# Attention inputs laid out by superchunk, with coarser routing steps and fp32 place tables

## The chip, the cores and the metric

The kernel runs on one core of a Trainium2 chip. A core has TensorE (matmuls), VectorE, ScalarE and GpSimd (elementwise work, each with its own queue of instructions), and SyncE (SP), which here only issues loads. The metric is the device time in microseconds; three runs of the kernel before gave 750.98, 752.05 and 753.02 us, median 752.05.

## The reference

Eight batches of 576 tokens with eight heads of 64 go through sliding-window attention, and each of the 4608 rows that come out (512 numbers) goes through one of eight experts. Which one depends on the token before it: a token keeps its predecessor's expert unless it is the first of its sequence or a local gate is below one half.

```python
mask = (rel >= 0) & (rel < 64)
scores = np.where(mask, scale * np.matmul(q, k.transpose(0, 1, 3, 2)), -1e9)
attn = softmax(scores)                      # per row
x = np.matmul(attn, v)                      # (B, S, H*D) after the bridge
logits = x @ w_gate                         # (B, S, 8)
local_gate = sigmoid(x @ w_local)           # (B, S)
# for each batch, token after token:
e = argmax(logits[b, s]) if s == 0 or local_gate[b, s] < 0.5 else prev_e
p = softmax(logits[b, s])
out[b, s] = p[e] * (relu(x[b, s] @ w1[e]) @ w2[e])      # 512 -> 1024 -> 512
```

All arithmetic is fp32.

## The kernel before, in words

**Attention** works on nine superchunks of 512 tokens (index `sc`), each with four head pairs (`hp`): 36 units. A unit is `scores` (L232 on: matmuls of keys against queries into PSUM, an exponential on ScalarE at L254, a multiplication p\*mask on VectorE at L257) and, two units later (LEAD = 2), `values` (L260 on: p against the values, L267; then on VectorE a reciprocal L272, the gate columns g L274 and the rows x L276). Once a superchunk, `gates` (L204) multiplies the transposed values `vtt` by the gate weights (L209), and `spread` (L215) transposes the result (L219) and puts it into the columns behind each head's values in `va` (L220), so that the value matmuls give the gate logits as well. Windows that start in the middle of a block of 128 need a second copy of the values shifted by 64 rows, `vb`; ScalarE makes it with five copies (L224, L227 to L230), two of them per unit.

**Loads** are issued on SP. `load(sc)` (L159) brings keys and queries into one tile of the pool `ring` (four buffers of 2 MB, which later hold expert weights) and the values into `va` (three buffers); `turned(sc)` (L171) brings `vtt` (one buffer). In memory, keys, queries and transposed values are [128, 4, 4608], so that a superchunk is four rows of 2 KB per partition; `v3` is [4608, 8, 74], four rows of 2368 B per partition. At the end of a superchunk, GpSimd issues the write of x to `xs` in memory (L322) and VectorE sums the gate columns into `lt` (L320).

**Routing** (`Router`) is written as generators that are advanced step by step between other work. `gate` (L554) does half of the tokens: argmax, the scan over tokens (transposes, scans on VectorE, transposes back), counts by matmuls with `ones` and `tri` (L628, L629), ranks. `first` (L734) then places the first half's tokens into six blocks of 128 and `second` (L766) all the rest into eight blocks of 256 and up to 21 of 128. `table` (L695) turns places into lists of tokens and weights: VectorE builds one-hot matrices for nine chunks of 128 tokens at a time (rowh L706; one L711; colh L716), TensorE multiplies them (L723), VectorE reads out `idx` and `pw` (L726 to L732). Before, the one-hot matrices are bf16; a token's number is split into two bf16 values and its weight into three (L656 to L659), five columns of values in all, and summed again at the end.

Each `yield` of these generators carries an estimate of VectorE's microseconds and whether a matmul follows that needs them. In attention, `step()` (twice a unit) advances `first` only when the estimate has been worked off at 0.8 us per call (HALF). In the experts, `step()` works off 3.5 us per call (STEP) and, when the account is empty, advances `second` up to the next matmul.

**Experts** (`Experts.run`, L897 on) go through 32 blocks: six of `first` (these are called quiet; ScalarE does all their PSUM reading), then 26 of `second`. `fetch` (L826) loads a block's two weight matrices (2 MB each, SP, L846) and gathers its rows (GpSimd, L840); `turn` transposes the rows (L859, L860), `hidden` does the first layer (L872) with the relu (L876, L878), `result` the second (L886), the scaling (L891) and the scattered write (L892). A step is taken after each group of `hidden` and twice per slot of `result`. A block is fetched two blocks ahead. Up to three more blocks may be needed; they are fetched and computed inside a conditional at the end, which these inputs do not enter.

**Order.** TensorE's instructions run as written (`manual_schedule`); the other engines' queues are ordered by the framework's scheduler, by priority in program order among what it takes to be ready. Each engine then runs its queue in order.

Of the kernel before, what the change touches and what calls it, by code (L numbers as in the profile page):

```python
# [11 lines left out]
BF16 = mybir.dt.bfloat16  # L12
# [7 lines left out]
P = 128  # L20
# [34 lines left out]
HALF = 0.8  # L55
STEP = 3.5
# [5 lines left out]
def kernel(  # L62
# [4 lines left out]
    v: bass.AP,  # L67
    v3: bass.AP,
# [30 lines left out]
    with ExitStack() as fast:  # L99
        ring = fast.enter_context(tc.tile_pool(name="ring", bufs=4))  # L100
        rt = Router(fast, tc, lt, tabs, ident)
        ex = Experts(fast, tc, ring, *moe)
        attention(tc, ring, q, k, v3, vt, xs, lt, ok, wg2s, ident, rt, ex)
        ex.run(fast, rt)
# [31 lines left out]
def attention(ctx, tc, ring, q, k, v3, vt, xs, lt, ok, wg2, ident, rt, ex):  # L136
# [22 lines left out]
    def load(sc):  # L159
        t = slice(sc * SC, (sc + 1) * SC)  # L160
# [4 lines left out]
        for i in range(0, HP, step):  # L165
            h = slice(i, i + step)
            nc.sync.dma_start(out=kt[:, h], in_=k[:, h, t])
            nc.sync.dma_start(out=qt[:, h], in_=q[:, h, t])
        nc.sync.dma_start(out=va, in_=v3[t].rearrange("(c p) h x -> p c h x", p=P))

    def turned(sc):  # L171
        vtt = vts[sc] = kp.tile([P, HP, SC], F32, name="vtt", bufs=1)
        nc.sync.dma_start(out=vtt, in_=vt[:, :, sc * SC:(sc + 1) * SC])
# [41 lines left out]
    def spread(sc, r, gs):  # L215
# [6 lines left out]
        vb = vbs[sc] = kp.tile([P, 4, H, VW], F32, name="vb", bufs=2)  # L222
        if sc:
            nc.scalar.copy(vb[WIN:, 0], vas[sc - 1][WIN:, 3])  # L224
        else:
            nc.gpsimd.memset(vb[WIN:, 0], 0.0)
        return [lambda: nc.scalar.copy(vb[:WIN, :2], va[:WIN, :2]),  # L227
                lambda: nc.scalar.copy(vb[WIN:, 1:3], va[WIN:, :2]),
                lambda: nc.scalar.copy(vb[:WIN, 2:], va[:WIN, 2:]),
                lambda: nc.scalar.copy(vb[WIN:, 3], va[WIN:, 2])]  # L230
# [50 lines left out]
    for move in spread(0, *gated):  # L281
        move()
    units = [(sc, hp) for sc in range(NSC) for hp in range(HP)]
    ps = {u: scores(*u) for u in units[:LEAD]}
    gated, moves = None, []
    side = None
    pause = 0

    def step():
        nonlocal pause  # L290
        if side and pause <= 0:
            pause = next(side, (0.0, False))[0]
        pause -= HALF

# [3 lines left out]
    for i, (sc, hp) in enumerate(units):  # L298
# [7 lines left out]
        if gated:  # L306
            moves = spread(sc + 1, *gated)
            gated = None
        for move in moves[:2]:
            move()  # L310
        moves = moves[2:]
        step()
# [5 lines left out]
        step()  # L318
# [173 lines left out]
class Router:  # L492
# [9 lines left out]
    def __init__(self, ctx, tc, lt, tabs, ident):  # L502
# [10 lines left out]
        self.iob = iota("iob", [1, NBLK, 1], [[1, NBLK], [0, 1]])  # L513
        pos = iota("pos", [P, G, GC], [[0, G], [P, GC]], 1)
# [14 lines left out]

        self.w = tl("w", P, C, 5, dt=BF16)  # L530
        nc.vector.tensor_copy(self.w[:, :, 0], iota("chunk", [P, C], [[1, C]], 0, -C))
        nc.vector.tensor_copy(self.w[:, :, 1], iota("at", [P, C], [[0, C]], 1))
# [21 lines left out]
    def gate(self, half, psum):  # L554

# [13 lines left out]
        yield 1.2, False  # L572
# [7 lines left out]
        yield 1.0, True  # L580
# [11 lines left out]
        yield 1.5, True  # L592
# [9 lines left out]
        yield 0.8, True  # L602
# [11 lines left out]
        yield 1.0, True  # L614
# [7 lines left out]
        yield 0.6, True  # L622
# [14 lines left out]
        yield 1.2, False  # L637
# [12 lines left out]
        yield 1.2, False  # L650
        pt = tl("pt", P, C1)
        vec.tensor_reduce(pt, pa, axis=AX.X, op=Alu.add)
        vec.tensor_tensor(pt, pt, sm, op=Alu.mult)

        w = self.w[:, cs]
        vec.tensor_copy(w[:, :, 2], pt)  # L656
        vec.tensor_tensor(pt, pt, w[:, :, 2], op=Alu.subtract)
        vec.tensor_copy(w[:, :, 3], pt)
        vec.tensor_tensor(w[:, :, 4], pt, w[:, :, 3], op=Alu.subtract)  # L659
# [35 lines left out]
    def table(self, psum, cs, ns, lo, hi, idx, pw):  # L695

        nc, last, vec = self.nc, self.last, self.nc.vector
# [3 lines left out]
        for a in range(0, n, 2 * m):  # L701
            built = []
            for b in range(a, min(a + 2 * m, n), m):
                rowh = self.oh_p.tile([P, m, P], BF16, name="rowh")
                sh = [P, m, P]
                vec.tensor_tensor(rowh, self.io128.to_broadcast(sh), last(lo[:, b:b + m]).to_broadcast(sh),  # L706
                                  op=Alu.is_equal)
                yield 1.3, False
                one = self.oh_p.tile([P, m, 1, NS], BF16, name="one")[:, :, :, :ns]
                sh = [P, m, ns]  # L710
                vec.tensor_tensor(one[:, :, 0], self.ios[:, :, :ns].to_broadcast(sh),  # L711
                                  last(hi[:, b:b + m]).to_broadcast(sh), op=Alu.is_equal)
                colh = self.oh_p.tile([P, m, 5, NS], BF16, name="colh")[:, :, :, :ns]
                sh = [P, m, 5, ns]
                w = self.w[:, cs.start + b:cs.start + b + m, :].rearrange("p c (k o) -> p c k o", o=1)
                vec.tensor_tensor(colh, one.to_broadcast(sh), w.to_broadcast(sh), op=Alu.mult)  # L716
                built.append((rowh, colh))
                yield 0.3 + 0.05 * ns, b + m >= min(a + 2 * m, n)
            if tab is None:
                tab = psum()[:, :5 * ns].rearrange("p (k s) -> p k s", k=5)  # L720
            for k, (rowh, colh) in enumerate(built):
                for i in range(m):
                    nc.tensor.matmul(tab, lhsT=rowh[:, i, :], rhs=colh[:, i], start=(a + k + i == 0),  # L723
                                     stop=(a + k * m + i == n - 1))
        t = self.tl("t", P, 5, NS)[:, :, :ns]
        vec.tensor_copy(t, tab)  # L726
        at = self.tl("at", P, NS)[:, :ns]
        vec.scalar_tensor_tensor(at, t[:, 0], float(P), t[:, 1], Alu.mult, Alu.add)
        vec.tensor_scalar(at, at, float(N), 0.0, Alu.add, Alu.max)
        vec.tensor_scalar(idx, at, float(N), None, Alu.min)  # L730
# [262 lines left out]
```

## Time and profile before

The profiled execution took 752.05 us; its span, from first to last instruction, is 750.2 us, at a mean granted TensorE clock of 0.981.

| | busy us | share of the span |
|---|---|---|
| TensorE matmuls | 691.8 | 92% |
| TensorE weight loads (beside them) | 502.4 | 67% |
| VectorE | 182.7 | 24% |
| ScalarE | 145.8 | 19% |
| GpSimd | 92.8 | 12% |

203.84 MB were moved. The busy share is an average over two stages of different kinds: attention (to 149 us), in which all engines work and the DMA engines are full, and the experts (161 to 742 us), in which TensorE never stops. A wait costs time only where it holds up the engine that sets the pace of its stage.

### The profile page before, as it was taken

Reading aid. Unit: us, or ns where it says so; the run is one execution under the profiler, and the core shown is the slowest. Engines: PE = TensorE matmul, PEld = TensorE weight load, DVE = VectorE, ACT = ScalarE, POOL = GpSimd, SP = SyncE. Lnnn points to the kernel's source line nnn. Section 1 sums busy time; section 2 is a strip of 40 time slices with the busy share of each in tenths; the row PEclk is TensorE's granted clock in tenths of the full one; section 3 lists DMA queues with packets and bytes.
Section 4 is the critical chain, followed back from the end, with each engine's and each line's share of the span. In section 5 each row is a group of like instructions: output and inputs, shape, how many; then the busy total and the mean of one; then the engine's idle time right before and its main releaser. Section 6 shows DMA issues by size and latency. Waiting matters only on the chain. (4 is left out here: it accounts for less than half of the span.)

```text
span 750.2 us, 12553 instructions
## 1 busy us (share of the span) xinstructions
PE 691.8 (92%) x5479; PEld 502.4 (67%) x5479; DVE 182.7 (24%) x426; ACT 145.8 (19%) x186; POOL 92.8 (12%) x109
## 2 busy tenths in 40 slices
PE   3788787749999999999999999999999999999995
PEld 2666666647677767567567567576776777677673
DVE  4576788923730011011010010010010001001000
ACT  2667665401111101101101101100110110010010
POOL 2000000111132111111110110111111111010010
PEclk9799999969999999999999999999999999999998
DMA  9999996867889964644654643689889898888601
GB/s 327 388 393 399 395 388 251 321 245 251 325 313 382 423 268 142 241 178 140 231 186 139 225 187 141 216 308 348 307 332 328 307 343 307 319 295 310 225 15 31
DMA packets 37331, 203.84 MB, mean 272 GB/s; under 512 B 3437, under 2 KB 3453, under 8 KB 29072
## 3 DMA queue, kind: packets, MB, share of 16 engines
q1 hardware_dynamic: 28320, 173.45, 63.1%
q0 software_dynamic: 8944, 29.45, 9.9%
q8 instruction: 47, 0.77, 0.4%
q14 instruction: 20, 0.16, 0.1%
HBM read 184.01 MB, written 19.92 MB: 272 GB/s over the span
## 5 line engine op out<-in xcount | busy, mean ns | idle before, releaser
L872 PEld LDWEIGHTS hp<-xt,w 128*128 128x128 f32 x2048 | 274.8, 193 | 28.3 <-issue 14.3
L872 PE MATMUL hp<-xt,w 128*128 128x128 f32 (+1 forms) x2048 | 289.9, 303 | 0.7 <-ACT xt L860 0.7
L886 PE MATMUL yp<-w,h 128*128 128x512 f32 x640 | 280.4, 592 | 0.0
L886 PEld LDWEIGHTS yp<-w,h 128*128 128x128 f32 x640 | 118.9, 190 | 136.8 <-issue 134.9
L876 DVE TENSOR_SCALAR h<-hp 128x512 f32<-128x512 f32 x34 | 23.5, 691 | 473.5 <-issue 362.0
L891 ACT ACTIVATE y<-yp,pw 128x512 f32<-128x512 f32 x40 | 27.5, 687 | 358.3 <-PE yp L886 342.2
L892 POOL DMA_INDIRECT out_dram<-y,idx x40 | 41.8, 1045 | 302.6 <-ACT y L891 275.8
L840 POOL DMA_INDIRECT xg<-xs,idx x40 | 39.1, 977 | 217.3 <-PE tp L859 188.4
L878 ACT ACTIVATE h<-hp 128x512 f32<-128x512 f32 x46 | 27.5, 597 | 163.0 <-PE hp L872 163.0
L238 PE MATMUL sp<-w 64*64 64x128 f32 (+1 forms) x1296 | 46.4, 278 | 13.7 <-issue 8.4
L238 PEld LDWEIGHTS sp<-w 64*64 64x64 f32 x1296 | 39.7, 142 | 22.8 <-issue 14.4
L267 PE MATMUL xo<-vb,p 128*64 128x74 f32 x576 | 46.8, 233 | 8.3 <-issue 4.3
L267 PEld LDWEIGHTS xo<-vb,p 128*64 128x64 f32 x576 | 40.8, 138 | 11.5 <-issue 4.8
L267 PE MATMUL xo<-va,p 128*64 128x74 f32 x576 | 47.0, 234 | 1.5 <-issue 1.5
L257 DVE TENSOR_TENSOR p<-p,mask 128x1024 f32<-128x1024 f32 x36 | 43.9, 1221 | 12.1 <-ACT p L254 11.9
L267 PEld LDWEIGHTS xo<-va,p 128*64 128x64 f32 x576 | 40.8, 138 | 2.7 <-issue 2.7
L254 ACT ACTIVATE p<-sp 128x1024 f32<-128x1024 f32 x36 | 36.7, 1022 | 15.7 <-PE sp L238 14.1
L859 PE MATMUL tp<-ident,xg 128*128 128x128 f32 x160 | 23.2, 277 | 10.8 <-DMA xg<-xs,idx 10.8
L859 PEld LDWEIGHTS tp<-ident,xg 128*128 128x128 f32 x160 | 18.9, 143 | 11.8 <-issue 11.0
L209 PE MATMUL xo<-vtt,wg2s 128*32 128x512 f32 x72 | 12.5, 705 | 13.9 <-DMA wg2s<-in_wg_dram 8.3
L276 DVE TENSOR_TENSOR x<-xo,allr 128x512 f32<-128x512 f32 x36 | 24.5, 680 | 0.0
L322 POOL DMA_DIRECT2D xs<-x x9 | 6.9, 764 | 130.3 <-DVE x L276 116.2
(198 smaller groups left out, 201.5 us busy)
## 6 DMA issues: line engine op xcount, KB each, us to landing
w<-in_w_dram SPq DMA_DIRECT2D x64, 2048.0 KB, 8.7
va<-in_v_dram SPq DMA_DIRECT2D x9, 1184.0 KB, 12.6
vtt<-in_vt_dram SPq DMA_DIRECT2D x9, 1024.0 KB, 11.1
xs<-x POOLq DMA_DIRECT2D x9, 1024.0 KB, 10.2
w<-in_k_dram SPq DMA_DIRECT2D x8, 1024.0 KB, 13.1
w<-in_q_dram SPq DMA_DIRECT2D x8, 1024.0 KB, 15.0
w<-in_k_dram SPq DMA_DIRECT2D x4, 256.0 KB, 6.1
w<-in_q_dram SPq DMA_DIRECT2D x4, 256.0 KB, 5.8
```

The source lines that it names most:

```text
L238: nc.tensor.matmul(sp[c * WIN:(c + 1) * WIN, j, a:b], lhsT=kt[h, hp, block * WIN:(block + 1) * WIN], rhs=qt[h, hp, a:b], start=True, stop= ...
L254: nc.scalar.activation(p, sp, Act.Exp, scale=DH ** -0.5)
L257: nc.vector.tensor_tensor(p, p, m.to_broadcast([P, 2, SC]), op=Alu.mult)
L267: nc.tensor.matmul(xo[par * WIN:(par + 1) * WIN, j, s * VW:(s + 1) * VW], lhsT=p[:, j, b * WIN:(b + 1) * WIN], rhs=w[:, s, 2 * hp + j, :], ...
L276: nc.vector.tensor_tensor(x[:, :, hp].rearrange("p c j d -> p j c d"), o[:, :, :, :DH], rr.to_broadcast([P, 2, 4, DH]), op=Alu.mult)
L840: nc.gpsimd.indirect_dma_start(out=x, out_offset=None, in_=self.xs[:rows, :], in_offset=bass.IndirectOffsetOnAxis(ap=idx[:, s:s + 1], axis=0))
L859: nc.tensor.transpose(tp[:, kk, :], x[:, kk * P:(kk + 1) * P], self.ident)
L872: nc.tensor.matmul(hp[:, i, :], lhsT=st["w1"][:, kk, m * P:(m + 1) * P], rhs=st["xt"][:, kk, :n], start=(kk == 0), stop=(kk == DK - 1))
L878: nc.scalar.activation(o, hp, Act.Relu)
L886: nc.tensor.matmul(yp, lhsT=st["h"][:, m, i * P:(i + 1) * P], rhs=st["w2"][:, m, :], start=(m == 0), stop=(m == FK - 1))
L891: nc.scalar.activation(y, yp, Act.Copy, scale=st["pw"][:, s:s + 1])
L892: nc.gpsimd.indirect_dma_start(out=self.out[:, :], out_offset=bass.IndirectOffsetOnAxis(ap=st["idx"][:, s:s + 1], axis=0), in_=y, in_offse ...
```

## The change

Four parts, in one diff.

1. Layout and loads. Keys and queries come as `kq`, [9, 128, 2, 4, 512]; values and transposed values are also laid out by superchunk. `load` issues one load for keys and queries (2 MB; for superchunk 0 four of 512 KB, one per head pair), with 16 KB in a row per partition, 9.5 KB for `va` and 8 KB for `vtt`. The plain `q`, `k`, `v` stay for the conditional part at the end of the kernel.
2. `vb` is copied by GpSimd in three copies right after `spread`, in place of ScalarE's five over two units.
3. Routing advances one `yield` at a time without accounts: in attention once per unit, in the experts at each call, the first of which now comes ahead of the first block's `turn`. There are fewer yields, only where a matmul follows or a large part ends. The one-hot matrices are fp32, with two columns of values (token, weight) in place of five; each piece takes one comparison for rowh, one for colh and two multiplications.
4. In the experts, blocks are fetched two ahead to the end of the list, and the three spare ones unconditionally; the conditional only computes them.

```diff
     def load(sc):
-        t = slice(sc * SC, (sc + 1) * SC)
         both = ring.tile([P, 2, HP, SC], F32, name="w")
...
-            nc.sync.dma_start(out=kt[:, h], in_=k[:, h, t])
-            nc.sync.dma_start(out=qt[:, h], in_=q[:, h, t])
-        nc.sync.dma_start(out=va, in_=v3[t].rearrange("(c p) h x -> p c h x", p=P))
+            nc.sync.dma_start(out=both[:, :, h], in_=kq[sc, :, :, h])
+        nc.sync.dma_start(out=va, in_=v3[sc])
...
-        nc.sync.dma_start(out=vtt, in_=vt[:, :, sc * SC:(sc + 1) * SC])
+        nc.sync.dma_start(out=vtt, in_=vt[sc])
...
+        nc.gpsimd.tensor_copy(vb[:WIN], va[:WIN])
+        nc.gpsimd.tensor_copy(vb[WIN:, 1:], va[WIN:, :3])
         if sc:
-            nc.scalar.copy(vb[WIN:, 0], vas[sc - 1][WIN:, 3])
+            nc.gpsimd.tensor_copy(vb[WIN:, 0], vas[sc - 1][WIN:, 3])
...
-        return [lambda: nc.scalar.copy(vb[:WIN, :2], va[:WIN, :2]),
-                lambda: nc.scalar.copy(vb[WIN:, 1:3], va[WIN:, :2]),
-                lambda: nc.scalar.copy(vb[:WIN, 2:], va[:WIN, 2:]),
-                lambda: nc.scalar.copy(vb[WIN:, 3], va[WIN:, 2])]
...
-        step()
         values(sc, hp, ps.pop((sc, hp)), x, g)
...
-        step()
+        if side:
+            next(side, None)
...
# Router.table, for each piece of nine chunks (each yield of gate, first and second loses its weights)
-                rowh = self.oh_p.tile([P, m, P], BF16, name="rowh")
+                rowh = self.oh_p.tile([P, m, P], F32, name="rowh")
...
-                colh = self.oh_p.tile([P, m, 5, NS], BF16, name="colh")[:, :, :, :ns]
-                vec.tensor_tensor(colh, one.to_broadcast(sh), w.to_broadcast(sh), op=Alu.mult)
-                yield 0.3 + 0.05 * ns, b + m >= min(a + 2 * m, n)
+                colh = self.oh_p.tile([P, m, 2, NS], F32, name="colh")
+                one = colh[:, :, 1, :ns]
+                eng.tensor_tensor(one, self.ios[:, :, :ns].to_broadcast(sh), last(hi[:, b:b + m]).to_broadcast(sh),
+                                  op=Alu.is_equal)
+                eng.tensor_tensor(colh[:, :, 0, :ns], one, last(self.tok[:, c]).to_broadcast(sh), op=Alu.mult)
+                eng.tensor_tensor(one, one, last(self.pt[:, c]).to_broadcast(sh), op=Alu.mult)
                 built.append((rowh, colh))
+            yield
...
# Experts.run
         def step():
-            nonlocal side, pause
-            pause -= STEP
-            if pause > 0.0:
-                return
-            pause, trip = 0.6, False
-            while side and not trip:
-                w, trip = next(side, (0.0, None))
-                pause += w
-                if trip is None:
-                    side = None
-                    late.append(self.fetch(0, spare=True))
+            nonlocal side
+            if side and next(side, self) is self:
+                side = None
+                late.append(self.fetch(0, spare=True))
...
-            n = order[i + 2] if i + 2 < total else 0
-            if n:
+            n = order[i + 2]
+            if n > 0 or n < 0:
                 jobs.append(self.fetch(n, spare=n > 0 and n % 3 == 0))
...
+        for n in order[total + 2:]:
+            jobs.append(self.fetch(n, spare=n % 3 == 0))
...
-            for n in order[total:]:
-                st = self.fetch(n, spare=n % 3 == 0)
+            for st in jobs[total:]:
                 self.turn(st, False)
```

## Prediction

> **What bounds the kernel now.** I read the 40 slices first, then ten-microsecond windows, TensorE's waits, and the timeline at the two seams. TensorE is busy 92% of the span and without a gap from 161 us to 742 us, so the expert stage is paid by TensorE alone: only what makes it wait there, or gives it more to do, counts. Attention (8 to 148.7 us) and the step into the experts (148.7 to 161.3 us) are where it idles.
>
> Windows; after the busy times of five engines come TensorE's granted clock, DMA share and GB/s:
>
> ```profile
> 50.00:60.00 10.00, 8.91 (x219) 6.91 (x214) 7.75 (x15) 5.98 (x7) 0.76 (x1) 1.00 1.05 395
> 120.00:130.00 10.00, 8.47 (x216) 6.83 (x215) 9.52 (x36) 6.12 (x8) 0.75 (x1) 1.00 0.46 149
> 240.00:250.00 10.00, 10.00 (x78) 8.97 (x77) 0.00 (x0) 2.85 (x5) 2.21 (x3) 1.00 1.01 431
> ```
>
> At 50 us the DMA engines are full at 395 GB/s with rows of 2 KB; at 240 us they are full with weight rows of 16 KB at 431 GB/s. From 120 us VectorE is the crowded engine (95%).
>
> But is attention late for data? What TensorE waited for from 40 to 95 us:
>
> ```profile
> PE xo L267 <- issue: 5.2, 4, 1.8
> PE sp L238 <- issue: 4.5, 4, 1.8
> PE xo L209 <- issue: 1.1, 1, 1.1
> PE xo L209 <- PE xo L267: 0.4, 1, 0.4
> ```
>
> No wait names a load. Nine gaps of "issue", 10.8 us, fall in the middle of runs of matmuls; otherwise the blocks touch (scores of a unit 1.05 us, values 1.19 us). So a superchunk is 10.6 us of TensorE (four units of 2.24, gates 1.0, transposes 0.6), 2.7 us of these gaps and some 0.4 of refilling after them: the 13.7 us between ends of superchunks.
>
> The seam to the experts, in the timeline:
>
> ```profile
> 146.34 0.62 PE L723 MATMUL xo<-colh,rowh 128*128 128x30 bf16 x18 [0.77 <-DVE x L276]
> 148.25 1.04 POOL L840 DMA_INDIRECT xg<-xs,idx  x1 [5.72 <-DVE idx L730]
> 159.50 1.08 PE L859 MATMUL tp<-ident,xg 128*128 128x128 f32 x4 [10.83 <-DMA xg<-xs,idx]
> 161.26 6.06 PE L872 MATMUL hp<-xt,w 128*128 128x128 f32 x32 [0.68 <-ACT xt L860]
> 167.37 3.74 PE L872 MATMUL hp<-xt,w 128*128 128x128 f32 x32
> ```
>
> The first place table is ready only in the last unit; its gather lands 11 us later beside weight loads, TensorE idles 10.83 us, and its clock then costs 6.06 - 3.74 = 2.3 us.
>
> The second routing, inside the experts:
>
> ```profile
> 182.76 0.41 PE L628 MATMUL r<-oh,ones 128*128 128x144 f32 x2
> 187.26 7.03 PE L886 MATMUL yp<-w,h 128*128 128x512 f32 x16
> 193.08 1.35 DVE L706 TENSOR_TENSOR rowh<-io,lo 128x1152 bf16<-128x1152 f32 x1
> 194.35 0.50 DVE L711 TENSOR_TENSOR one<-ios,hi 128x333 bf16<-128x333 f32 x1
> 205.15 1.64 PE L723 MATMUL r<-colh,rowh 128*128 128x185 bf16 x18
> ```
>
> VectorE needs until 193.1 us from the counts of 182.8 us to begin the table; the pauses put the table's matmuls at 205.2 us, well behind it.
>
> [...] 47 packets of 0.77 MB on the instruction queue, gaps roughly every 128 load-and-multiply pairs; so I read "issue" as instruction fetch beside full DMA engines. [...]
>
> **The change part by part**, against the profiled 752.05 us (span 750.2, 1.85 around it; its run is also the median of the three).
>
> *Loads.* Bytes per superchunk stay: 2048 + 1024 + 1184 KB in, 1024 KB of x out, 5.41 MB. At 395 GB/s that is 13.7 us, at about 425 (the rows out stay 2 KB) 12.7. So at most 1.0 us per superchunk, 5 us over the five before VectorE crowds. I take -1.0: no wait names data, and the fetch gaps were as long (0.72 and 1.29 us at 133 and 139 us) beside weight loads of 16 KB rows; the DMA engines stay nearly full at any pace TensorE can reach. Range -5 to +2[...]. One SP issue in place of two: 2.5 to 4 us less of SP per superchunk, but SP waits for buffers anyway; without that cover it would be 1 us of landing.
>
> *vb copies from ScalarE to GpSimd.* Three copies of 2368, 1776 and 592 elements. GpSimd's memset of 592 took 0.627 us, so I estimate 5.0 us in all per superchunk, against 4.9 on ScalarE. At the start ScalarE's copies (15.7 to 20.0 us) held the first exponential and TensorE for 5.38 us; values of unit 0 then began at 23.0. On GpSimd they end near 20.7, beside the exponentials: -1.8 (first gates load allowing; 0 to -2.3). Later they are due 8 us after va's columns: covered, but p*mask (1.22 us, two SBUF inputs) waits for a copy of up to 2.5 us. In superchunks 0 to 4 VectorE's 9.5 us of 13.7 and the lead of two units (3.5 us) cover it: +1.0 (0 to +3).
>
> *First routing, one step a unit.* Eight steps from unit 20 give the table at unit 27 of 36, not 35. VectorE's 17 us of routing (summed from L565 to L730 without the pieces removed) fall in two superchunks: 18.4 own + 17.0 + 5.0 for half of the GpSimd time blocked = 40.4, at the best share seen (95%) 42.5, less 3.5 of lead, against 31.4 between those ends before: +7.6. The last two superchunks lose their VectorE waits (2.4) and the table's matmuls (0.6): +4.6 net. Without blocking it is -0.6 (35.4 for 40.4); with all of it and more bubbles +10. f32 matmuls of the first table (36 records of at most 0.115 us) hide in those waits.
>
> *Seam.* Table, gather and both weights of the first block (buffers of superchunks 5 and 6, free at units 25 and 29) are in before attention ends, so tp, copy and hp follow at once, 1.3 us: -11.0, and a warm clock, -2.3. Together -13.3 (0 if the gather stays late). xs (row write of the last superchunk) and the second block's weights are due 14 us later.
>
> *Second routing, one step per call.* Calls come every 3.7 us as now until 182.8 us; then rest of gate, places and table take three calls. TensorE would want the first 18 table matmuls in the middle of result of block 2, 190.9 us. VectorE begins the table at 193.1 as before, and a piece is rowh 1.27 + three of 0.41 = 2.5 to 2.7 us: first piece 195.8, second 198.4. TensorE waits 5 us, does nine, waits 0.7, does nine: over at about 200.2, 9.3 us. The other half is ready in time: 3.2 us. An f32 table matmul is two records; 74 columns at the 0.88 ns per column of L886 are 0.065, at most the 0.115 us of L872's records, so 36 take 4.7 to 8.3, I take 6.4. Against 2 x 1.48 before: 12.5 - 2.95 = +9.6. [...] +2.3, as at the seam. +11.9 (8 to 15). Queued behind the waiting matmuls is all of TensorE's expert work, so nothing hides it. The bf16 splits (L656 to L659) go, but they fill VectorE's wait for L628: 0.
>
> *End.* Three spare blocks (12 MB, 3 gathers) are now fetched unconditionally. Every load needed is ahead of them on SP, and 4 MB per 14.45 us is the rate anyway: 0. But the last w2 waits for the last result's buffer (742.1 us) and lands 7.9 us later at best, with 0.3 for SP and 0.6 beside the last rows out, against a last landing near 750: +1.3 (0 to +4).
>
> Sum: -1.0 - 1.8 + 1.0 + 4.6 - 13.3 + 11.9 + 1.3 = +2.7, so 754.8 us.
>
> **Rivals.** (a) *GpSimd's copies hold VectorE throughout.* For: p*mask and most routing steps have two SBUF inputs. Against: half of VectorE's work reads PSUM. With all 5 us blocked a superchunk needs 14.5 us of VectorE, over 13.7: four superchunks at +0.8 and +4 more in the crowded two: 762. It decides from 4.2 us blocked per superchunk. (b) *Ends faster:* the copies block nothing (-0.6 in place of +4.6, 0 in place of +1.0: 748.6), at best with the loads' whole 5 us instead of 1: 744.6. I price it 746.5; it decides when less than about 1 us per superchunk is blocked. (c) *No change:* the loads give nothing, but TensorE keeps its clock in the table wait and the f32 matmuls run at the low price (+8 in place of +11.9): 751. (d) *The gather stays late,* queued on GpSimd behind x's writes: +13.3, 768. Against: two gathers were issued ahead of the last write before.
>
> **How the numbers follow.** This kernel's runs can't tell 0.3% (2.3 us) from no change: faster is below 749.8, slower above 754.3. Forecast 0.45 (own range 750 to 760: faster 0.03, same 0.15, slower 0.27); (a) 0.20 slower; (b) 0.20 faster; (c) 0.10 same; (d) 0.05 slower. So 0.23, 0.25, 0.52. From 746 to 764 leaves out half of (b) and all of (d) and the top of (a), about 0.2.
>
> **What would show it.** Right: tp (L859 before) within 2 us of the last values; one TensorE wait of 4 to 7 us on a VectorE piece of the table near 190 us and a slow stretch after it; GpSimd copies of about 2.5, 1.9 and 0.6 us; DMA near 420 GB/s in attention with "issue" gaps still there; a last w load landing after 749 us. Wrong: attention ending before 145 us (b) or after 156 us (a), p*mask stretched or late by copies; a gather landing after attention (d); no wait at the second table (c).

## The result, and the profile after

The changed kernel took 777.64 us (median of four runs, 776.95 to 779.68) against 751.51 us for the kernel before on the same chip. The ratio is 1.0355 with a 95% interval of 1.0321 to 1.0389: 24 to 29 us slower. The forecast was 754.8 us, range 746 to 764; the direction was right, the size far too small.

The profiled execution has a span of 775.2 us against 750.2 us. Both are divided at the same events (the first three rows are times from the span's start); the last matmul is the small transpose of a flag (L129 before, L127 after) that follows the last expert block.

| | before | after | difference |
|---|---|---|---|
| first gates matmul of superchunk 6 | 95.86 | 94.91 | -1.0 |
| attention's last values | 148.67 | 160.64 | +12.0 |
| first expert matmul | 161.26 | 161.85 | +0.6 |
| from there to the last matmul | 581.4 | 597.5 | +16.0 |
| from there to the span's end | 7.5 | 15.9 | +8.4 |
| span | 750.2 | 775.2 | +25.0 |

The same windows as before, with one more behind 120 us (busy time of five engines, TensorE's granted clock, DMA share, GB/s):

```profile
50.00:60.00 10.00, 9.16 (x236) 7.48 (x234) 7.38 (x14) 4.12 (x5) 4.45 (x3) 1.00 1.00 394
120.00:130.00 10.00, 1.21 (x32) 1.06 (x32) 9.96 (x34) 0.41 (x1) 1.43 (x2) 0.65 0.55 193
130.00:140.00 10.00, 9.52 (x72) 9.52 (x72) 1.52 (x9) 0.00 (x0) 0.43 (x1) 0.50 0.31 123
240.00:250.00 10.00, 10.00 (x75) 8.65 (x74) 0.00 (x0) 1.65 (x3) 1.00 (x1) 1.00 1.01 426
```

At 50 and 240 us little has changed. The loss of attention lies in one place: from 120 to 130 us TensorE works 1.2 of 10 us while VectorE is full, and from 130 to 140 us TensorE is "busy" at half clock with only 72 matmuls. (The trace's clock records have it at half from 122.9 to 143.4 us, and again from 194.6 to 208.2 us.) TensorE's timeline shows what that is, and the two other stages that the prediction priced:

```profile
130.48 7.83 PE L691 MATMUL xo<-colh,rowh 128*128 128x12 f32 x36 [9.27 <-DVE colh L683]
138.24 1.99 PE L232 MATMUL sp<-w 64*64 64x128 f32 x36
...
161.85 3.81 PE L834 MATMUL hp<-xt,w 128*128 128x128 f32 x32 [1.21 <-ACT xt L822]
...
195.85 7.93 PE L691 MATMUL r<-colh,rowh 128*128 128x74 f32 x36 [6.65 <-DVE colh L684]
203.58 5.96 PE L848 MATMUL yp<-w,h 128*128 128x512 f32 x8
209.38 4.14 PE L691 MATMUL r<-colh,rowh 128*128 128x74 f32 x36
```

The first table waits 9.27 us for VectorE's pieces, then takes 7.83 us where the bf16 table took 0.62, and a unit's scores after it take 1.99 us in place of 1.1. The seam is as forecast: the wait of 10.83 us for the gathered rows is gone, and the first 32 records take 3.81 in place of 6.06 us. The second table waits 6.65 us and takes 7.93 and 4.14 us.

The end, in the timeline of all engines, before:

```profile
742.42 0.27 PE L129 MATMUL op<-ident,ok 128*1 128x128 f32 x1 [0.30 <-PEq L946]
742.73 0.28 DVE L131 TENSOR_REDUCE lo<-op 1x1 f32<-1x128 f32 x1 [6.69 <-PE op L129]
```

and after:

```profile
759.04 0.27 PE L127 MATMUL op<-ident,ok 128*1 128x128 f32 x1 [0.64 <-PEq L901]
768.01 0.28 DVE L129 TENSOR_REDUCE lo<-op 1x1 f32<-1x128 f32 x1 [15.69 <-DMA w<-in_w_dram]
```

Before, VectorE reduces the flag 0.04 us after the matmul. After, it waits 8.7 us more, for the landing of the last spare block's weights; what follows the flag takes 7.5 us before and 7.2 us after. So the landing is in series with the flag. Why the flag's small tile waits for a tile of weights, the trace doesn't say. In the kernel its pool is opened after the experts' pools are closed, so it may stand in their place; no run tests that.

### The profile page after: what moved, and what is told of

It reads as the page before. It is cut to its first block, busy times and chain, and to the rows that moved or that the text cites. A ratio compares the mean times of both kernels' runs of the same rounds, so it can differ in the third digit from the quotient of the medians.

```text
span 775.2 us, 12649 instructions
## 1 busy us (share of the span) xinstructions
PE 708.4 (91%) x5533; PEld 517.8 (67%) x5533; DVE 186.8 (24%) x415; ACT 103.1 (13%) x142; POOL 152.1 (20%) x137
## 4 chain that ended last, share of the span: by engine, by line
PE 85%; DVE 7%; DMA 4%; issue 2%; ACT 0%; POOL 0%; DVEq 0%; POOLq 0%; ACTq 0%
PE hp L834 36%; PE yp L848 35%; PE sp L232 4%; PE xo L261 4%; PE tp L821 2%; DMA vtt<-in_vt_dram 2%; DVE p L251 2%; PE r L691 2%; PE xo L205 1%; DMA w<-in_w_dram 1%; PE xo L691 1%; DVE x L270 1%; DMA wg2s<-in_wg_dram 1%; DVE rowh L675 1%; PE xo L215 1%
## 5 line engine op out<-in xcount | busy, mean ns | idle before, releaser
L848 PE MATMUL yp<-w,h 128*128 128x512 f32 x640 | 282.8, 596 | 0.0
L848 PEld LDWEIGHTS yp<-w,h 128*128 128x128 f32 x640 | 119.9, 192 | 138.2 <-issue 136.3
L802 POOL DMA_INDIRECT xg<-xs,idx x43 | 42.1, 979 | 224.2 <-PE tp L821 199.9
L251 DVE TENSOR_TENSOR p<-p,mask 128x1024 f32<-128x1024 f32 x36 | 52.0, 1449 | 10.9 <-ACT p L248 10.7
L219 POOL COPY vb<-va 64x2368 f32<-64x2368 f32 x9 | 26.9, 2986 | 46.6 <-DVE va L216 46.6
L205 PE MATMUL xo<-vtt,wg2s 128*32 128x512 f32 x72 | 11.8, 736 | 13.3 <-DMA wg2s<-in_wg_dram 9.1
L822 DVE COPY xt<-tp 128x512 f32<-128x512 f32 x32 | 21.2, 680 | 0.0
```

The costliest lines, as they stand in the source:

```text
L251: nc.vector.tensor_tensor(p, p, m.to_broadcast([P, 2, SC]), op=Alu.mult)
L802: nc.gpsimd.indirect_dma_start(out=x, out_offset=None, in_=self.xs[:rows, :], in_offset=bass.IndirectOffsetOnAxis(ap=idx[:, s:s + 1], axis=0))
L848: nc.tensor.matmul(yp, lhsT=st["h"][:, m, i * P:(i + 1) * P], rhs=st["w2"][:, m, :], start=(m == 0), stop=(m == FK - 1))
```

## Experiments

Microseconds "by ratio" are (ratio - 1) x 752. The theory after these traces: four losses that are nearly separate, namely f32 tables on TensorE's path, VectorE's work handed over in large pieces, GpSimd's copies, and the fetches at the end; the layout gives nothing. The rival was the forecast's (a), GpSimd's lock on VectorE throughout.

**The layout alone**, put into the kernel before:

```diff
-            nc.sync.dma_start(out=kt[:, h], in_=k[:, h, t])
-            nc.sync.dma_start(out=qt[:, h], in_=q[:, h, t])
+            nc.sync.dma_start(out=both[:, :, h], in_=kq[sc, :, :, h])
# va and vtt as in the change, the arrays too
```

> The kernel before with only the new layout and the joined load of keys and queries. Account from the two traces: attention never waits for data, so 749 to 752 us, the fetch gaps of TensorE staying at about 2.7 us per superchunk. Rival (the loads set attention's pace): 746 us or less, with attention ending 5 us earlier. Rival (long rows delay instruction fetch): over 754 us, with longer gaps of 'issue'.

751.5 us, ratio 0.9985 (0.9969 to 1.0001): no change that can be told, at most 2.3 us of gain. From 50 to 90 us the DMA engines moved 411 GB/s in place of 396, and the gaps of "issue" from 40 to 95 us stayed (11.0 us against 10.8): attention did not wait for data, so data that comes sooner is worth nothing. That these gaps are instruction fetch, as the prediction reads them, is an estimate: the page of before has 12553 instructions and 47 packets on the instruction queue, 267 to a packet, near the 256 of 128 load-and-multiply pairs; no trace has the times of these packets.

**The spare fetches back inside the conditional**, in the kernel after:

```diff
-            n = order[i + 2]
-            if n > 0 or n < 0:
+            n = order[i + 2] if i + 2 < total else 0
+            if n:
...
-        for n in order[total + 2:]:
-            jobs.append(self.fetch(n, spare=n % 3 == 0))
...
-            for st in jobs[total:]:
+            for n in order[total:]:
+                st = self.fetch(n, spare=n % 3 == 0)
```

> The changed kernel with the three spare blocks fetched inside the conditional, as before. If the flag at the end waits for the last spare weight load, the time falls by the 8.7 us that the end grew, to 769 us, and the flag's reduction follows its transpose within 1 us. If the end is long for another reason (gathers, the drain), it falls by less than 3 us.

769.44 us, ratio 1.0252 (1.0214 to 1.0289). The flag's line is that of before again, in the timeline of this kernel:

```profile
758.25 0.28 DVE L129 TENSOR_REDUCE lo<-op 1x1 f32<-1x128 f32 x1 [6.69 <-PE op L127]
```

**The same part alone**, the fetches taken out of the conditional in the kernel before (the diff is the reverse):

> The kernel before with the spare weights fetched ahead of the conditional block and nothing else. If the flag's tile waits for the last weight's landing as it does in the kernel after: 15 to 18 us from the last matmul to the span's end in place of 8.1, and 758 to 761. If that loss needs the rest of the change: 751 to 753.

760.95 us, ratio 1.0113 (1.0081 to 1.0145), +8.5 by ratio. In its timeline:

```profile
743.08 0.27 PE L129 MATMUL op<-ident,ok 128*1 128x128 f32 x1 [0.61 <-PEq L948]
751.49 0.28 DVE L131 TENSOR_REDUCE lo<-op 1x1 f32<-1x128 f32 x1 [15.10 <-DMA w<-in_w_dram]
```

Put in or taken out, it is about 8 us, and nothing else of the change is needed for it. That it is shown both ways settles which part lengthens the end.

**Both tables' matmuls three steps later**, in the kernel after:

```diff
-            yield
+            for _ in range(wait if a == 0 else 1):
+                yield
# wait is a new argument of table(), 4 for both tables
```

> The changed kernel with three more yields between the building of each table's first pieces and the matmuls that read them; nothing else. If the two TensorE waits (9.3 and 6.7 us) and the half clock after them (about 7 and 6 us) are the loss, the time falls by 22 to 29 us, to 749 to 756 us, and the gather of the first block is still early. If the waits only move, because VectorE is short of time whatever the order (GpSimd's copies), it falls by less than 12 us, with a wait of similar length at the new place.

763.57 us, ratio 1.0160 (1.0127 to 1.0193). The second wait is gone and its two halves take 4.14 us each at full clock; first expert matmul to last matmul is 585.6 us in place of 597.5. Attention ends at 160.33, as in the kernel after. But superchunk 6 began 2.6 us later here (97.53 against 94.91 us), before any step that the edit moves, so the ends mislead: counted from its first gates, attention takes 62.8 us in place of 65.7 (52.8 in the kernel before). That is little for a wait of 9.27 us gone. The long wait became shorter ones for VectorE and issue (0.9, 1.8, 2.0 and 2.2 us between 121 and 137 us), and the clock was at half for 20.5 us once more (128.7 to 142.3 us, and 145.7 to 152.6 us from within the table). So of 22 to 29 expected, the second routing's part came, and of the first's only some 3 us.

**The first routing in shorter pieces as well**:

```diff
         vec.tensor_tensor(base, run, te, op=Alu.subtract)
+        yield
...
         vec.tensor_tensor(pa, pa, oh, op=Alu.mult)
+        yield
# and three more, two in first() and one in table(); gate() and table() serve the second routing too;
# first table's matmuls one step later, not three
```

> The kernel after with both tables' matmuls put later, and with further steps in the first routing, so that VectorE gets it in shorter pieces, one for each unit's scores. If attention's loss of 12.0 us is VectorE handed too much at once in units 24 to 28: gates(8) moves from 142.3 back to about 130 to 135, attention's last values from 160.6 to 145 to 152, and the time from 763.6 (late matmuls alone) to 750 to 757. If VectorE is simply short of time there, wherever the pieces stand: attention still ends at 158 to 161 and the time is 760 to 765. If the table now comes too late for the gather: attention ends early, but the experts' first matmul stays at 160 or later, behind a wait for the gathered tile.

767.19 us, ratio 1.0187 (1.0160 to 1.0214): missed. The first half of the expectation came true (gates of superchunk 8 at 128.96 us in place of 142.32), and still attention ended at 159.43. Superchunk 6 had begun 3.7 us later than in the kernel after; from there attention takes 60.8 us, 4.9 less than in the kernel after and still 8.0 more than before. Much of that time reappeared at the table: it ran at 148.24 us for 5.89 us after a wait of only 0.41, and the clock was 0.52 from 150 to 160 us. The table also came too late for the gather, which was waited for again (3.46 us, first expert matmul at 164.69). So VectorE's crowding is not the whole loss of attention; why the clock falls at the table is asked below.

**bf16 tables in the kernel after**, still one step per call:

```diff
-                rowh = self.oh_p.tile([P, m, P], F32, name="rowh")
+                rowh = self.oh_p.tile([P, m, P], BF16, name="rowh")
# colh with five bf16 columns, the splits of token and weight and their sums, as before
```

> The kernel after with the bf16 tables of before (five columns for each row in place of two), still at one routing step for each call. If the place tables' matmuls in f32 cost what the trace of after shows (4.1 us warm and 7.9 us cold for 36, against 1.5 warm before): 4 to 6 us less in the second routing and about 5 less in the first, 765 to 770. If the waits ahead of the tables are the cost and the matmuls' type is not: the waits stay at 9 and 6.7 us and the time stays at 774 to 779. VectorE has more to write for the bf16 tables (five columns), which could eat 2 to 4 us of the gain.

764.88 us, ratio 1.0167 (1.0146 to 1.0187), 14 us less by ratio than the kernel after. TensorE's timeline:

```profile
131.37 0.42 PE L699 MATMUL xo<-colh,rowh 128*128 128x30 bf16 x9 [9.16 <-DVE colh L692]
...
189.96 1.57 PE L699 MATMUL r<-colh,rowh 128*128 128x185 bf16 x9 [7.12 <-DVE colh L692]
```

Both waits stand, 9.16 and 7.12 us, yet attention ends 6.4 us earlier (154.28; 7.2 us less from superchunk 6 on) and the experts' stretch is 5.8 us shorter. VectorE isn't the reason, for it does more for the bf16 pieces (18.9 us in all against 15.3). So about half of the loss (14 of 26.7 us) is the tables' own time, 7.83 and 12.07 us, with the waits ahead of them unchanged.

**f32 tables in the kernel before**, with its spacing (the reverse of that diff):

> The kernel before with the f32 place tables alone; the spacing, ScalarE's copies, the layout and the end stay. If the tables cost by themselves what after_bf16 gave back: attention's last values some 5 to 7 us later (153 to 156), the experts some 4 to 6 us longer, and 759 to 765. If the f32 tables are dear only where TensorE has idled just before and its clock is halved: 36 records of 0.115 in place of 0.041 us each, 2.7 us for each half of 36, which makes 5 in the second routing and 2 to 3 in attention, partly behind the gather's wait: 754 to 759.

755.92 us, ratio 1.0046 (1.0033 to 1.0058), +3.5 by ratio. Attention ends 5.6 us later (154.27), but the wait for the gathered rows falls from 10.83 to 3.25 us, so the first expert matmul is 2.0 us earlier; the experts' stretch is 4.5 us longer. The first table's line, in TensorE's timeline:

```profile
146.65 5.45 PE L716 MATMUL xo<-colh,rowh 128*128 128x12 f32 x36 [0.72 <-DVE allr L272]
```

There was next to no wait, and yet 36 records take 5.45 us, where two halves of the second table take 4.14 each. Windows of 1.7 us (columns as above, the clock third from the end) show why:

```profile
147.10:148.80 1.70, 1.70 (x18) 1.70 (x17) 0.39 (x1) 0.00 (x0) 0.00 (x0) 1.00 0.98 414
148.80:150.50 1.70, 1.70 (x13) 1.70 (x12) 0.00 (x0) 0.00 (x0) 0.00 (x0) 0.64 0.93 395
150.50:152.20 1.70, 1.70 (x10) 1.67 (x12) 0.06 (x1) 0.00 (x0) 0.00 (x0) 0.50 1.07 443
```

TensorE is busy without a gap and its clock falls to a half all the same. The 74-column table keeps 1.00. Is it the number of columns?

**The first table with 74 columns** in that kernel, 68 of which nobody reads:

```diff
-        yield from self.table(psum, slice(0, C1), FIRST, lo, hi, tabs["idx1"], tabs["pw1"])
+        yield from self.table(psum, slice(0, C1), NS, lo, hi, tabs["idx1"], tabs["pw1"])
# in table(): the yields keep the estimate of 12 columns, and idx and pw read the first six of 37 places
```

> The kernel before with f32 tables, and 74 columns in the first table in place of 12 (68 of them are not used); the pacing is unchanged. If few columns bring the clock down: the table takes 4.1 to 4.2 us in place of 5.45, the clock stays at 1.00 through it and the values after it take 1.3 us in place of 2.2; attention's last values at 151.5 to 153 in place of 154.3, and the time 0 to 3 us less than with 12 columns (752 to 756), since VectorE writes some 3 us more. If the gaps before the table do it: the clock falls to half during the table again, which takes 5 us or more, and the time is 756 to 760.

The line, and the windows:

```profile
145.54 4.21 PE L716 MATMUL xo<-colh,rowh 128*128 128x74 f32 x36 [0.57 <-DVE allr L272]
```

```profile
146.00:148.00 2.00, 2.00 (x20) 2.00 (x20) 0.38 (x1) 0.00 (x0) 0.00 (x0) 1.00 0.95 391
148.00:150.00 2.00, 2.00 (x25) 1.92 (x26) 0.21 (x2) 0.00 (x0) 0.00 (x0) 1.00 1.09 459
```

Six times the columns, 1.2 us less time, full clock; the values after it take 1.25 in place of 2.24 us. Attention ends at 150.94, earlier than expected, but superchunk 6 had also begun 1.9 us earlier; from there the gain is 1.5 us. The time is the same (755.62, ratio 1.0049, 1.0030 to 1.0068), for the gather's wait grows again, to 6.67 us.

**The same in the kernel with late matmuls:**

> The kernel after with late matmuls and 74 columns in the first table. If few columns bring the clock down: the table takes 4.1 to 4.2 us in place of 5.17 and the next scores and values 1.1 and 1.3 in place of 2.0 and 2.2; attention ends 2 to 4 us earlier than 160.3, and the time is 759 to 763 (763.6 with 12 columns). If the gaps do it: 5 us or more for the table and 763 to 768.

The table in TensorE's timeline of the kernel with late matmuls:

```profile
142.76 5.17 PE L692 MATMUL xo<-colh,rowh 128*128 128x12 f32 x36
```

and in this one:

```profile
144.76 4.24 PE L692 MATMUL xo<-colh,rowh 128*128 128x74 f32 x36
```

The clock, which falls within the first, is 1.00 all through the second; the scores and values after it take 1.12 and 1.25 us: the same as in the pair before. Attention gains nothing (160.16): VectorE's longer pieces (0.50 us in place of 0.21 for each part of colh) stand ahead of the x that TensorE waits for at 137 us, and that wait grows from 2.2 to 4.5 us. The time is 762.3 us, ratio 1.0137 (1.0090 to 1.0183), not to be told from 763.57. That few columns bring the clock down is so shown in two kernels, by one profiled execution of each; why they do is not. Nor is the clock what held attention up in this kernel.

**ScalarE's copies in the kernel after:**

```diff
-        nc.gpsimd.tensor_copy(vb[:WIN], va[:WIN])
...
+        return [lambda: nc.scalar.copy(vb[:WIN, :2], va[:WIN, :2]),
# and so on, two per unit, as before
```

> The changed kernel with vb copied by ScalarE in pieces, as before. If GpSimd's copies hold VectorE and so make the first table late, the masks fall from 1449 to about 1225 ns on average and the first wait (9.3 us) shrinks by 2 to 4 us and attention by 3 to 6 us: 772 to 775 us. If they are the main cause of that wait: it goes below 3 us and the time below 768. If they are covered: 777 us.

776.23 us, ratio 1.0347 (1.0315 to 1.0379): no difference from 1.0355 that can be told, though attention ends 2.2 us earlier and the first table's wait is 6.2 in place of 9.3 us.

**GpSimd's copies alone in the kernel before** (the reverse):

> The kernel before with the shifted value tiles copied by GpSimd alone, all at the place of the other spread steps; layout and routing stay those of before. My forecast's rival, that GpSimd's copies hold VectorE's, would make it 757 to 764, with the masks' mean up from 1221 to 1400 ns or more. The kernel after with ScalarE's copies was only 1.4 us quicker, by which this one stands at 750 to 754. If ScalarE's load was worth something: 746 to 750.

758.41 us, ratio 1.0084 (1.0060 to 1.0109), +6.3 by ratio, against my expectation and as the forecast's rival (a) had it. Groups of that kernel (line, engine, operation, count, then busy time and mean ns):

```profile
L255 DVE TENSOR_TENSOR p<-p,mask 128x1024 f32<-128x1024 f32 x36 | 52.0, 1449 | 7.5 <-ACT p L252 7.4
...
L223 POOL COPY vb<-va 64x2368 f32<-64x2368 f32 x9 | 27.0, 3001 | 51.9 <-DVE va L220 51.9
```

p\*mask takes 1449 ns on average in place of 1221. TensorE's waits for VectorE from 84 to 168 us, the two longest groups:

```profile
PE xo L265 <- DVE x L274: 5.7, 4, 2.3
PE xo L265 <- DVE cnt L633: 4.0, 1, 4.0
```

Attention ends at 154.87, and the gather, now also late, is waited for as before (9.6 us). The copies and the masks exclude each other, as a pair of this kernel shows (GpSimd's timeline, then VectorE's):

```profile
88.32 3.09 POOL L223 COPY vb<-va 64x2368 f32<-64x2368 f32 x1 [5.30 <-DVE va L220]
...
90.97 1.52 DVE L255 TENSOR_TENSOR p<-p,mask 128x1024 f32<-128x1024 f32 x1 [0.60 <-ACT p L252]
```

The copy's end is at 91.41 us and the mask's 1.08 us after it. So it is with all ten masks that took over 1.3 us: each ends 1.08 us after the end of the copy that had started before it. In the kernel after the same copies cost little, probably because the long table wait comes last there anyway; no run separates that.

**The spacing alone taken away** from the kernel before:

```diff
-        nonlocal pause
-        if side and pause <= 0:
-            pause = next(side, (0.0, False))[0]
-        pause -= HALF
+        if side:
+            next(side, None)
# once per unit, with the steps and the experts' step() of the change
```

> The kernel before with the spacing alone taken away: one routing step for each call in attention and in the experts, steps as large as those of after; bf16 tables, ScalarE's copies and the layout stay. From the three parts measured so far: attention's last values are 12.0 us later in after than before; 6.4 of it went with the bf16 tables and 2.2 with ScalarE's copies, which leaves 3.4 for the spacing: attention ends at 151 to 153, the first expert matmul loses its wait for the gather, the second routing costs some 10 to 13, and the time is 748 to 754. If the spacing is the whole cause of attention's loss and tables and copies only act through it: attention ends at 156 or later and the time is 758 or more.

756.22 us, ratio 1.0063 (1.0038 to 1.0088), +4.7 by ratio: between the two expectations. Attention +6.4 (waits of 7.7 us and 0.6 us at the first table), seam -11.3, the experts' stretch +8.7 (7.1 and 1.05 at the second table).

**The same with the new layout:**

> The kernel before with the new layout and without the spacing. If the layout's earlier superchunks are what let the four-part kernel's attention end at 149.8: attention ends at 149 to 151 here, against 155.1 with the old layout, and the time is 749 to 752. If the 5 us were chance between executions: 153 to 156 and 754 to 758, as without the layout.

756.74 us, ratio 1.0060 (1.0041 to 1.0079). In the profiled execution, the fastest of the eight runs, attention ended 3.5 us earlier than with the old layout, but the runs show no gain. Single ends of attention differ by some 2 to 4 us between executions, so differences of that size prove nothing by themselves.

**Four parts of the kernel after undone or moved** (bf16 tables, ScalarE's copies, fetches in the conditional, second table's matmuls three steps later), and **the same with the first table two steps later**. Their diffs are those above.

> The kernel after with four parts undone at once: bf16 tables, ScalarE's copies, the spare fetches inside the conditional block again, and the second table's matmuls three steps later. If the parts add as read one by one: attention ends at 152 to 153, the first expert matmul at 153 to 154, the experts take 581 to 583 up to the last matmul as before, and the end takes 8: a span of 742 to 745 and a time of 743 to 747, below both kernels. If they overlap, so that undoing one leaves another's loss in place: 750 or more.

> The same with the first table's matmuls two steps later as well. If the 9 us for which TensorE waits for the first table's pieces are a loss of attention: 3 to 6 us less than without it, 738 to 743. If VectorE's work sets attention's end, the wait only spreads, as it did with the f32 tables: within 2 us of the kernel without it, or more if the gather becomes late.

745.79 us, ratio 0.9935 (0.9910 to 0.9961), and **743.36 us, ratio 0.9897 (0.9875 to 0.9920)**: both are faster than both kernels, and the second is hardly to be told from the first. They keep of the change the layout and the coarse steps without accounts. In the profiled executions attention ends at 149.8 and 151.2 us, the first expert matmul follows at 151.1 and 152.6 (161.3 before), and the experts' stretch is 581.1 us in both, as before. (The first profile is of the fastest of nine runs, 4.1 us under their median.) The first table's wait of 7.8 us, which the second kernel no longer has, was worth 1.4 us of attention there, counted from superchunk 6. The second's whole list of TensorE's waits from 150 to 742 us:

```profile
PE hp L853 <- ACT xt L841: 1.4, 1, 1.4
PE r L706 <- DVE colh L698: 1.0, 1, 1.0
PE tp L840 <- issue: 0.5, 1, 0.5
PE op L128 <- PEq L918: 0.4, 1, 0.4
PE xo L264 <- DVE allr L269: 0.3, 1, 0.3
```

No wait for the gather is left: its table is ready early enough.

**The routing's account worked off faster** in the kernel before with the new layout (HALF of 0.95 and of 1.1 in place of 0.8):

> The kernel before with the new layout and the place in the scan at which the first list is cut moved from 0.8 to 0.95 of the unit's share, so that the first list's routing is issued about as far along but its gather is awaited by more of attention. If the wait for the gathered tile of 8.8 to 10.8 us before the experts is set by where the first table stands: it changes by more than 2 us and the time goes to 741 to 748, or up by as much. If that wait is set by something else: 749 to 753.

> The kernel before with the new layout and the routing's steps taken 1.4 times as fast as there (a credit of 1.1 for each call in place of 0.8). With 0.95 the gather was issued 2.6 us earlier than with 0.8 and landed no earlier, at about 748.7. If an earlier gather is worth its time: issued at 138 to 141 with a wait of under 5 before the experts, 742 to 746. If VectorE's time sets it: attention loses what the gather gains, 748 to 752.

HALF is what each call works off the account, not a place in the scan, as the first expectation has it; and the 748.7 of the second is the time of the run with 0.95, not that of a landing. 748.75 us (ratio 0.9950, 0.9920 to 0.9980) and 747.29 us (0.9946, 0.9926 to 0.9965). The gather's wait is 9.2 and 8.9 us, no less than the layout's own 8.8: it was issued at 144.4 and 145.1 us in place of 147.0 and landed at 155.8 and 154.8 in place of 156.1. The profiled spans, 747.0 and 747.6 us, are that of the layout alone, 747.2, but they are of unlike executions: that of the layout alone was 2.3 us under the median of its runs, that of 1.1 was 2.4 us over. So there is a small gain in the runs that the traces don't explain; it stays open.

## Why the prediction was wrong

Its sum against the same terms in the traces:

| term | predicted | measured |
|---|---|---|
| loads, start, early superchunks | -1.8 | -1.0 |
| first routing, to attention's end | +4.6 | +13.0 |
| seam | -13.3 | -13.6 |
| second routing | +11.9 | +18.3 |
| end | +1.3 | +8.4 |
| sum | +2.7 | +25.0 |

*Loads: right, as far as can be told.* -1.0 for the layout was measured as -1.1 by ratio (-2.3 to +0.1).

*Start: the gain of 1.8 did not come,* by an exception like the one that it named (a gates load). Values of unit 0 began at 19.3 us, 3.7 earlier, and then TensorE waited 4.14 us for the second `vtt`, so the second gates began at 26.64 us against 26.38.

*GpSimd's copies: the size came out, in part by luck.* The prediction put 6.2 us to their blocking, an estimate, since no trace of the kernel before shows any: the +1.0 of the early superchunks, and the 5.2 between -0.6 and +4.6 in the first routing. Alone in the kernel before they cost 6.3. But the forecast was for the kernel after, and there undoing them gives back 0.6 by ratio, each interval reaching 2.5 us to either side, and 2.2 us of attention's end in the profiled execution. The copies took 3.0, 2.3 and 1.3 us on average, where 2.5, 1.9 and 0.6 had been estimated. The prediction's signs of rival (a), attention ending after 156 us and p\*mask stretched, both appeared in the kernel after, and taken by themselves would have misled: the lateness came from the tables.

*First routing: this step failed.* The sentence was that the first table's f32 matmuls "hide in those waits". They can't: the wait is for the pieces that those matmuls read, so they come after it, and with them all of attention that TensorE has queued behind. They took 7.83 us, where the forecast put nothing, and the scores and values after them 1.8 us more than at full clock; together 9.6, which covers the 8.4 missing. With bf16 tables 6.4 of it came back at once: from superchunk 6 on, attention then takes 5.7 us more than before, near the +4.6 that was forecast without the tables' time. With ScalarE's copies as well, and nothing else changed in attention (the four-part kernel), its end was at 149.8 us, 10.9 earlier than in the kernel after; but 2.8 of these had come before superchunk 6. The price was the second mistake: at most 0.115 us for each record, which holds only at full clock; at half clock it was 0.217 us.

*Seam: right,* both halves: 11.4 of idle time and 2.25 of slow clock. But the first was no gain of its own. The kernel before idles 10.8 us there, and after fills that time with a longer attention; f32 tables alone likewise moved attention's end by +5.6 and the experts' beginning by -2.0.

*Second routing: mechanism right, one term too small.* Waits: 5.7 forecast, 6.65 measured. Clock after the idle time: 2.3 forecast (that of the seam, after 10.83 us idle; that 5 us would bring it too was an estimate), 2.4 measured after 6.65 us (5.96 less 3.60 us for the eight matmuls of L848). The tables: 6.4 forecast for 72 records, 12.07 measured. I took a middle between a price by columns (0.065 us) and that of full records (0.115); the upper end was right at full clock (4.14 us for 36), and the half clock, which I priced only for what follows, doubled the first half to 7.93. At full clock the traces have 115 ns a record in the second table and 117 in the widened first one, both with 74 columns, and 117 for L872's records of 128 columns before (3.74 us for 32): the price by columns was the wrong one.

*End: this step failed.* The landing itself was priced well (issue at 758.43 us, 9.2 us to land), but as one landing beside the last scatter. The flag stands behind it, and 7.2 us of further work behind the flag: +8.4.

*The parts together.* Alone in the kernel before they cost -1.1 (layout), +6.3 (copies), +4.7 (spacing), +3.5 (f32 tables) and +8.5 (fetches), 21.9 of the 26.7 by ratio; the other 4.8 is about what the intervals leave open (0.9 to 2.6 us to either side for each). That the parts interact shows where they are undone instead: without the spacing TensorE idles before each table (9.27 and 6.65 us in the kernel after) and the f32 records then run at half clock (0.217 us each in the first table, 0.220 in the first half of the second, against 0.115 at full clock), and the tables that cost 3.5 alone give back 14 in the kernel after; the copies that cost 6.3 alone give back nothing that can be told. Which of rival (a) and my theory held is thus a matter of place: (a) is true of the kernel before and nearly idle in the kernel after.

## What to carry to other kernels

A matmul that waits for a piece can't hide in that wait: add its own time, at the clock that the wait leaves (0.50 here after 9.27 and 6.65 us), and the time of all that is queued behind it. When an unconditional transfer is moved to the end, look for the small final step that waits for it, not for the bandwidth. Take a bundle apart both ways, each part alone in the old kernel and each undone in the new: the two prices of the f32 tables (3.5 and 14 us) and of the copies (6.3 and about 0) are both true.

## What the runs showed of the hardware

- In a stream of f32 matmuls with only 12 columns on 128-column weights TensorE's clock fell to a half while the trace has it busy: 2.1 to 3.0 us after the first record in three kernels, whose 36 records take 5.2 to 5.9 us; with 74 columns, in two of these kernels, the clock stays at 1.00 and they take 4.2. The busy time doesn't tell the two apart (1.70 of 1.70 us at a clock of 0.50, 2.00 of 2.00 at 1.00); what sets the clock the runs don't show.
- At half clock the f32 table cost nearly the same with 12 columns (7.83 us) as with 74 (7.93): the columns did not set its time. The profile has the weight loads busy as long as the matmuls (9.52 us of TensorE's 9.52 between 130 and 140 us); whether they set it the trace doesn't show.
- GpSimd's copies and VectorE's p\*mask, whose inputs both lie in SBUF, run one after the other: the one that starts second is done 1.08 us (p\*mask) or 2.01 us (copy of 64 x 2368) after the end of the first (kernel before with GpSimd's copies). So that copy took 2.1 to 3.2 us, 3.0 on average, and p\*mask 1449 ns on average in place of 1221. VectorE's x, which reads PSUM, is not held up: in the kernel after, 11 of the 30 between 10 and 150 us lie wholly within a copy and took 0.67 to 0.68 us, as the others did.
